# Key-value products and remainder rows moved into other runs of the TensorE stream (linear attention and a gated feed-forward on one core)

## The chip, the cores and the metric

The kernel runs on one core of a Trainium2 chip. The core has a matrix engine (TensorE, PE in the profile, with PEld for its weight loads), a vector engine (VectorE, DVE), a scalar engine (ScalarE, ACT), a general engine (GpSimd, POOL), a queue engine that mostly issues transfers (SyncE, SP), and 16 DMA engines that all queues share. The metric is the device time of one execution in microseconds (us), lower is better. Measured times are medians of several executions; a profile is one execution of its own.

## The reference

Eight batches, eight heads, 576 positions, 64 elements per head. Each batch and head computes a linear attention, is normalized over its 64 elements, and all 4608 rows of 512 then go through a normalized, gated feed-forward layer of width 1536:

```
kv  = einsum('bhsd,bhse->bhde', k, v)
out = einsum('bhsd,bhde->bhse', q, kv)
x   = out / sqrt(mean(out*out, -1) + 1e-6) * g_norm      # per head, then (b, s, h*d)
xn  = x / sqrt(mean(x*x, -1) + 1e-6) * rms_g             # per row
y   = (silu(xn @ w_gate) * (xn @ w_val)) @ w_out
```

Inputs and output are float32; the kernel multiplies in bfloat16 and sums in float32.

## The kernel before

**Tiling.** The 576 rows of a batch are cut into 512 main rows (`MAIN`, four chunks of 128, `NC = 4`) and a remainder of 64 (`REM`). The feed-forward works on eight groups of main rows, one per batch, and on one group of the 8 x 64 remainder rows. In its order the group of the remainder rows stands before that of the last batch. Code counts batches from 0 (`b`, `g`); the words here count from 1.

**A group** has 24 slots of its first half, gate and value in turn for each of the 12 column blocks `j` (`gate_of`, `val_of`, four matmuls of 512 columns each through `mm1`, L762), and 16 slots of its second half (`slots_b`, three matmuls each, L811). ACT applies silu to a gate (L771), DVE multiplies it with the value (L783), ACT copies the result of the second half (L831) and SP stores it (L833). The slots are the frame: `Placer.put` books the attention work of the next batch into the slots of the current group by estimated costs per engine, and `emit` writes out slot by slot. Each engine then runs its own instructions in that order, and waits only for semaphores.

**Attention of batch b** (`place_attention`, L669) is booked into group `b-1` (from 0): the transpose of q by SP (`qT_dma`, L381, and L384 for a pair of remainders), the k-v products on PE (`kv_mm`, L294, 40 matmuls whose results take half of the columns), their copy to `kvs` by DVE (`kv_half`, L324), o on PE (`o_heads`, L422, 32 matmuls that contract over half of the rows). Then come ACT's square and copy of o (`sq_`, `outa_`), POOL's weighted square (`wsq`, L514), DVE's sums (`red`, L522), a chain of twelve small DVE operations (`chain`, L562 to L580) that gives the scale `al`, the scaling (`xna_`, L591) and the transposes of x by SP (`x_dma`, L653) into the tile that the next group reads.

**Remainders.** The o of two batches' remainders is one more chunk (`o_rem`, L397) in the run of o of batches 3, 4, 6 and 8, with its squares and copies in halves (L405, L410), and a fifth column in the chain. The k-v products of batches 5 and 6, and of 7 and 8, form one run of 80 in the second half of the group before.

**PSUM** has three pools of tiles: `mm1` with three buffers, `o2` with two, `att` with three. A matmul that opens a tile waits until the last reader of its buffer is done.

**Loads.** POOL issues the loads of k and v with a cast (`load_cast`, L196 and L200) into two buffers each (`kc`, `vc`), SP those of q (`load_q`), which POOL or ACT casts. All waits of POOL and SP are in the order of their queues.

**The first two batches** are written out by hand. Batch 1's rows are made in two parts: its first group runs on the early half, while the late half is still scaled. `behind(n)` adds to the early slot `n`; at `n == 9` PE turns the late rows (L621) and ACT copies them out (L631). Batch 2 (`place_second`) sits in the first group's second half: four matmuls `oT` (L472), their squares on ACT (`sqT_`, L483), and sums over heads by small matmuls with a selection matrix (`stat_mm`, L507, four per `j`), then a chain on DVE (`lead_chain`) that scales its o.

Of the kernel before, what the change touches and what calls it, by code (L numbers as in the profile page):

```python
# [87 lines left out]
def kernel(  # L88
# [38 lines left out]
    xna_p = pool("xna", 2)  # L127
    x_p = pool("x", 3)
# [30 lines left out]
    q01r = consts.tile([2 * REM, H, D], BF16, name="q01r")  # L159
# [29 lines left out]
    def load_cast(b, t, heads=None):  # L189
        to = qc if t == 0 else (vc if t == 2 else kc)[b % 2]  # L190
        if heads is None:
            if t == 0:
                to = q01r[b * REM : (b + 1) * REM]
# [69 lines left out]
    class Att:  # L263
        def __init__(self, b):
            self.b = b
            self.kv, self.qT = kvs[b % 2 if b else 2], qTs[b % 2]
            self.chunks = NC + (b == 2 or b > 2 and b % 2)
            if b < 2:
                self.qTj = self.qT.rearrange("p c j t -> p (c j t)").rearrange("p (j c t) -> p j c t", j=NS, c=NC + 1)
            else:  # L270
                self.qTj = self.qT.rearrange("p c j t -> p j c t")
# [49 lines left out]

        def kv_half(self, half):
            rows, cols = slice(half * D, (half + 1) * D), slice(half * D, (half + 1) * D)
            nc.vector.tensor_copy(out=self.kv[rows, :, half, :], in_=self.kv_ps[rows, :, cols])  # L324
# [54 lines left out]
        def qT_dma(self):  # L379
            flat = mains[self.b, 0].rearrange("p c h d -> p (c h d)")  # L380
            nc.sync.dma_start_transpose(out=self.qT[:, 0:NC].rearrange("p c j t -> p (c j) t"), in_=flat)  # L381
            if self.chunks > NC:
                rem = q01r if self.b == 2 else rems[0][self.b // 2 % 2]
                nc.sync.dma_start_transpose(out=self.qT[:, NC], in_=rem.rearrange("p h d -> p (h d)"))  # L384

        def o_rem(self):

            of = (kvs[2], kvs[1]) if self.b == 2 else (kvs[0], kvs[1])
            self.o[NC] = [
                pool_.tile([128, H // 2, D], FP32, name=name) for pool_, name in ((att_p, "att"), (mm1_p, "mm1"))  # L390
            ]
            for j in range(NS):
                for n in range(2):
                    at = slice(n * REM, (n + 1) * REM)
                    for half in range(2):
                        rows = slice(half * D, (half + 1) * D)
                        nc.tensor.matmul(  # L397
                            self.o[NC][half][at, j, :], lhsT=self.qTj[rows, j, NC, at],
                            rhs=of[n][rows, j, half, :], start=True, stop=True, skip_group_check=True,
                        )  # L400

        def sq_rem(self, half):
            if NC not in self.sq:
                self.sq[NC] = sq_p.tile([128, 2, H, D], BF16, name="sq")
            nc.scalar.activation(out=self.sq[NC][:, 0, half:H:2, :], in_=self.o[NC][half], func=ACT.Square)  # L405

        def outa_rem(self, half):
            if NC not in self.outa:
                self.outa[NC] = outa_p.tile([128, H, D], BF16, name="outa")
            nc.scalar.copy(out=self.outa[NC][:, half:H:2, :], in_=self.o[NC][half])  # L410

        def o_heads(self):
# [5 lines left out]
            for c in range(NC):  # L418
                for j in range(NS):
                    for half in range(2):  # L420
# [3 lines left out]
                            rhs=self.kv[rows, j, half, :], start=True, stop=True, skip_group_check=True,  # L424
# [4 lines left out]
        def part(self, t, n):  # L429

            if n >= NC:
                return t[:, n]
# [12 lines left out]
        def xna_pairs(self, o, js, c0, c1):  # L445
            if not hasattr(self, "xna"):
                self.xna = xna_p.tile([128, NC + 1, H, D], BF16, name="xna")
# [6 lines left out]
        def o_of(self, c):  # L454
            return self.o[c] if c >= NC else self.o["main", c].rearrange("p c h d -> p (c h) d")
# [47 lines left out]
        def stat_mm(self, c0, c1):  # L503
            self.st = st = att_p.tile([128, 2, NC + 1, H], FP32, name="att")
            for c in range(c0, c1):
                for j in range(NS):
                    nc.tensor.matmul(  # L507
                        st[:, :, c, 2 * j : 2 * j + 2], lhsT=self.sqT[:, j, c], rhs=sel,
                        start=c == c0 and j == 0, stop=c == c1 - 1 and j == NS - 1,
                        skip_group_check=True,  # L510
                    )

# [3 lines left out]
        def red(self, c, which):  # L516
            if self.st is None:
                self.st = stat.tile([128, 2, NC + 1, H], FP32, name="st")
            of = self.sq[c][:, which]
            if c < NC:  # L520
                of = of.rearrange("p (c h) d -> p c h d", c=2)
            nc.vector.reduce_sum(out=self.part(self.st[:, which], c), in_=of, axis=AX.X)  # L522

        def chain_t(self):
            if not hasattr(self, "al"):
                t = lambda n, dt=FP32, h=H: stat.tile([128, NC + 1, h], dt, name=n)
                self.u, self.r, self.t, self.z, self.nt, self.al = (t(n) for n in ("u", "r", "t", "z", "nt", "al"))
                self.s = stat.tile([128, NC + 1], FP32, name="srow")
# [57 lines left out]
        def xna_(self, c, eng):  # L586
            if not hasattr(self, "xna"):
                self.xna = xna_p.tile([128, NC + 1, H, D], BF16, name="xna")
            if c < NC:
                of = self.o["main", c] if self.b == 1 else self.outa[c].rearrange("p (c h) d -> p c h d", c=2)  # L590
                return eng.tensor_tensor(  # L591
                    out=self.part(self.xna, c), in0=of,
                    in1=self.part(self.al, c).to_broadcast([128, 2, H // 2, D]), op=OP.mult,
                )
            return eng.tensor_tensor(
                out=self.xna[:, c], in0=self.outa[c], in1=self.al[:, c, :].to_broadcast([128, H, D]), op=OP.mult
# [48 lines left out]
        def x_dma(self, c0, c1):  # L645
# [3 lines left out]
            else:  # L649
                b = self.b // 2 * 2 if self.b > 2 else 0  # L650
                to = xr[:, :, b * REM : (b + 2) * REM]
                of = self.xna[:, NC].rearrange("p h d -> p (h d)")
# [16 lines left out]
    def place_attention(P, b, casts=(), at=0, chain_at=0, mate=None):  # L669
# [3 lines left out]
        N1 = range(a.chunks)  # L673
        P.floor = max(P.floor, at)
        load = P.put("SP", 0.0, a.qT_dma, casts[:1] if b == 2 else casts)
        qt = [("DMA", load[1] + QT_SLOTS)]
        if kv is None:
            of = [a] + ([Att(mate)] if mate else [])
            p = P.psum(1.2, lambda: [o.kv_mm(ALL) for o in of], casts, len(of))
            out_ = [[P.put("DVE", 0.4, lambda o=o, h=h: o.kv_half(h), [p]) for h in range(2)] for o in of]  # L680
            for tile_, ops in zip(P.tiles[-len(of) :], out_):
                tile_ += ops
            kv = out_[0]
            if mate:
                ahead[mate] = of[1], out_[1]
        else:
            P.floor = max(P.floor, start + 2)
        outs, reds = {}, []
        rem = a.chunks - NC
        main = P.psum(0.73 + 0.25 * rem, a.o_heads, kv + qt, 2 + rem)  # L690
        for c in (*N1[NC:], *N1[:NC]):
            if c == NC:
                for n in (1, 0):
                    s = P.put("ACT", 0.38, lambda n=n: a.sq_rem(n), [main])
                    outs[c] = P.put("ACT", 0.38, lambda n=n: a.outa_rem(n), [main])
                P.tiles[-1] += [s, outs[c]]
            else:
                s = P.put("ACT", 0.6, lambda c=c: a.sq_(c), [main])
                outs[c] = P.put("ACT", 0.6, lambda c=c: a.outa_(c), [main])
                if c >= 2:  # L700
                    P.tiles[c - NC - rem] += [s, outs[c]]
            assert outs[c][1] < start + 2 * NF, (b, outs)
            w = P.put("POOL", 1.2, lambda c=c: a.wsq(c, nc.gpsimd), [s])
            reds.append(P.put("DVE", 0.68, lambda c=c: a.red(c, 0), [s]))
            reds.append(P.put("DVE", 0.68, lambda c=c: a.red(c, 1), [w], w[1] + 3 * (b == 2)))
        prev = reds
        for n in range(0, 13, 4):
            prev = [P.put("DVE", 0.8, lambda n=n: [f() for f in a.chain(0, a.chunks)[n : n + 4]], prev, chain_at)]
        xn = [P.put("DVE", 0.68, lambda c=c: a.xna_(c, V), prev + [outs[c]]) for c in N1]
        put = [P.put("SP", 0.0, lambda c=c: a.x_dma(*c), [xn[c[1] - 1]]) for c in ((0, 2), (2, 4), (4, 5))[: a.chunks - 2]]  # L710
        return put[2 if b == B - 1 else 1][1] + X_SLOTS

    def place_second(P, s):
# [24 lines left out]
        P.at("PE", 0.5, lambda: a.stat_mm(0, NC), s + 5)  # L738
# [34 lines left out]
    def gate_of(g, j, c0=0, c1=MAIN):  # L773
        silu_of(g, j, mm1(g, wg, j, c0, c1, "o2" if g == 0 and c0 == 0 and j == 5 else "mm1"), c0, c1)
# [231 lines left out]
    G.memset(kvs[0], 0.0)  # L1006
# [20 lines left out]
    def behind(n):  # L1027
# [99 lines left out]
```

## Time and profile before

| | |
|---|---|
| median of 3 runs | 317.39 us (317.2 to 317.48) |
| profiled execution, its own time | 317.45 us |
| its span, first to last instruction | 315.7 us |
| granted TensorE clock | 1.000 |
| PE busy | 310.6 us, 98% of the span |
| DVE, ACT, POOL busy | 167.6, 139.1, 87.4 us |
| read from and written to memory | 37.78 MB, 9.44 MB |

The profile's page lists busy time by engine, the chain of work that ended last (followed back from the last instruction, at each step to what released it), and the costliest groups of instructions by source line. The chain can also be shown in order of time: start, length, engine, tile and line, with neighbouring pieces of the same line merged and their number behind an x. The timeline shows instructions of each engine with start, length and, in brackets, the idle time before them and what ended it. Matmuls are pipelined, so their starts are spaced more closely than they are long; the chain shows the spacing. For a DMA the landing is the time from issue to arrival.

### The profile page before, as it was taken

To read this page: it belongs to the slowest core of one execution; us is meant where nothing else is said; L and a number is where in the kernel's file an instruction comes from. 1 tells how busy PE (TensorE), PEld (TensorE's weight loads), DVE (VectorE), ACT (ScalarE), POOL (GpSimd) and SP (SyncE) were. 2 spreads that over 40 slices of the span, in tenths; PEclk is the share of its full clock that TensorE was granted. 3 is DMA by queue.
4 is the path that set the end of the run, shared out by engine and by line. 5 is a ranking of instruction groups with operands and counts; after the bars stand their busy time and mean duration, and the time that the engine had idled before them with its cause. 6 is when DMAs were issued, how large, how long until landed. Compare 5 with 4: busy or idle time off the path is not lost.

```text
span 315.7 us, 5706 instructions
## 1 busy us (share of the span) xinstructions
PE 310.6 (98%) x2220; PEld 154.8 (49%) x2220; DVE 167.6 (53%) x375; ACT 139.1 (44%) x261; POOL 87.4 (28%) x108
## 2 busy tenths in 40 slices
PE   8999999999999999999999999999999999999996
PEld 3688655544444445444444454444444444444444
DVE  4585456579669643955196638570769034103410
ACT  2374474595487324632483228322842233233321
POOL 8846430077068205830081007100510000000000
PEclk9999999999999999999999999999999999999999
DMA  9999999999899968997423444424001600040002
GB/s 199 194 203 199 196 237 200 192 231 147 190 162 215 179 152 140 253 175 163 166 85 67 94 135 141 83 48 152 3 0 25 194 1 0 21 105 9 2 33 100
DMA packets 78358, 40.18 MB, mean 127 GB/s; under 512 B 43000, under 2 KB 73852, under 8 KB 78332
## 3 DMA queue, kind: packets, MB, share of 16 engines
q0 software_dynamic: 32304, 14.75, 36.5%
q1 hardware_dynamic: 45328, 24.48, 31.6%
q10 hardware_dynamic: 700, 0.59, 0.6%
q8 instruction: 17, 0.28, 0.3%
q14 instruction: 9, 0.07, 0.1%
HBM read 37.78 MB, written 9.44 MB: 150 GB/s over the span
## 4 chain that ended last, share of the span: by engine, by line
PE 94%; DMA 2%; DVE 1%; POOL 1%; issue 1%; ACT 0%; DVEq 0%; POOLq 0%
PE mm L762 58%; PE o L811 27%; DMA vc<-in_v_dram 2%; PE mm L811 2%; PE att L294 2%; PE o L422 1%; PE o L842 1%; PE att L422 1%; PE att L472 1%; DVE h L783 0%; PE att L621 0%; PE mm L804 0%; PE o L762 0%; PE att L397 0%; PE mm L312 0%
## 5 line engine op out<-in xcount | busy, mean ns | idle before, releaser
L783 DVE TENSOR_TENSOR h<-silu,mm 128x512 bf16<-128x512 bf16 (+1 forms) x114 | 73.9, 650 | 101.1 <-PE mm L762 92.4
L771 ACT ACTIVATE silu<-mm 128x512 bf16<-128x512 f32 (+1 forms) x115 | 65.1, 570 | 83.5 <-PE mm L762 73.1
L762 PE MATMUL mm<-x,wv 128*128 128x512 bf16 (+1 forms) x408 | 97.7, 364 | 0.0
L762 PE MATMUL mm<-x,wg 128*128 128x512 bf16 (+1 forms) x404 | 97.5, 364 | 0.1
L811 PE MATMUL o<-wo,h 128*128 128x512 bf16 x396 | 89.6, 379 | 0.0
L762 PEld LDWEIGHTS <-wv 128*128 128x128 bf16 x468 | 45.1, 98 | 46.2
L762 PEld LDWEIGHTS <-wg 128*128 128x128 bf16 x456 | 44.4, 98 | 47.5 <-issue 0.4
L811 PEld LDWEIGHTS <-h 128*128 128x128 bf16 x420 | 40.6, 98 | 47.6
L514 POOL TENSOR_TENSOR sq<-sq,g 128x512 bf16<-128x512 bf16 x28 | 32.0, 1155 | 99.1 <-ACT sq L405 67.4
L831 ACT COPY osb<-o 128x512 f32<-128x512 f32 x33 | 19.3, 587 | 68.7 <-PE o L811 66.7
L522 DVE TENSOR_REDUCE st<-sq 128x8 f32<-128x512 bf16 x56 | 35.9, 678 | 0.0
L591 DVE TENSOR_TENSOR xna<-outa,al 128x512 bf16<-128x512 bf16 x24 | 15.1, 684 | 0.0
L324 DVE CAST kvs<-att 64x256 bf16<-64x256 f32 x14 | 5.9, 422 | 16.8 <-PE att L294 16.6
L200 POOL DMA_DIRECT2D kc<-in_k_dram x7 | 6.5, 924 | 29.0 <-PE att L294 26.1
L762 PE MATMUL mm<-xr,wg 128*128 128x512 bf16 x48 | 12.3, 379 | 0.0
L762 PE MATMUL mm<-xr,wv 128*128 128x512 bf16 x48 | 12.3, 379 | 0.0
L229 POOL CAST main_q<-stg 128x1024 bf16<-128x1024 f32 x10 | 10.1, 1043 | 1.2 <-DMA stg<-in_q_dram 1.2
L929 ACT ACTIVATE wv<-wv,gain 128x384 bf16<-128x384 bf16 x16 | 9.0, 607 | 0.4 <-PE mm L762 0.4
L200 POOL DMA_DIRECT2D vc<-in_v_dram x10 | 8.5, 857 | 2.1 <-PE att L294 1.1
L258 PE MATMUL mm<-idle 128*128 128x512 bf16 x20 | 7.2, 533 | 1.2 <-DVE idle L138 1.2
L811 PE MATMUL mm<-wo,h 128*128 128x512 bf16 x24 | 7.6, 379 | 0.0
L459 ACT ACTIVATE sq<-att 128x512 bf16<-128x512 f32 x12 | 7.5, 626 | 0.0
(151 smaller groups left out, 190.1 us busy)
## 6 DMA issues: line engine op xcount, KB each, us to landing
out_dram<-osb SPq DMA_DIRECT2D x27, 256.0 KB, 2.5
stg<-in_q_dram SPq DMA_DIRECT2D x6, 1024.0 KB, 11.2
vc<-in_v_dram POOLq DMA_DIRECT2D x7, 512.0 KB, 13.1
kc<-in_k_dram POOLq DMA_DIRECT2D x7, 512.0 KB, 7.8
out_dram<-osb SPq DMA_DIRECT2D x17, 128.0 KB, 2.4
wg<-in_moe_w_gate_dram POOLq DMA_DIRECT2D x4, 384.0 KB, 10.1
wv<-in_moe_w_val_dram POOLq DMA_DIRECT2D x4, 384.0 KB, 11.3
wo<-in_moe_w_out_dram POOLq DMA_DIRECT2D x4, 384.0 KB, 14.4
```

The source lines that it names most:

```text
L200: return nc.gpsimd.dma_start(out=to[:, heads[0] : heads[1], : NC * D], in_=view)
L229: return copy(out=mains[b, t][:, cs[0] : cs[1], h0:h1, :], in_=staged[b, t].rearrange("p h (c d) -> p c h d", c=NC)[:, cs[0] : cs[1], h0:h ...
L459: nc.scalar.activation(out=self.sq[c][:, 0], in_=self.o_of(c), func=ACT.Square)
L514: eng.tensor_tensor(out=self.sq[c][:, 1], in0=self.sq[c][:, 0], in1=g2, op=OP.mult)
L522: nc.vector.reduce_sum(out=self.part(self.st[:, which], c), in_=of, axis=AX.X)
L591: return eng.tensor_tensor(out=self.part(self.xna, c), in0=of, in1=self.part(self.al, c).to_broadcast([128, 2, H // 2, D]), op=OP.mult,)
L762: nc.tensor.matmul(ps[:, : c1 - c0], lhsT=w[n][:, s, jj * 128 : (jj + 1) * 128], rhs=x_of(g, s, c0, c1), start=s == 0, stop=s == NS - 1)
L771: nc.scalar.activation(out=sis[g, j][:, c0:c1], in_=ps, func=ACT.Silu)
L783: nc.vector.tensor_tensor(out=hs[g, j][:, c0:c1], in0=sis[g, j][:, c0:c1], in1=v_ps, op=OP.mult)
L811: nc.tensor.matmul(ps, lhsT=hs[g, j][:, t * 128 : (t + 1) * 128], rhs=wo[j // OB][:, j % OB, :], start=j == 0, stop=j == NF - 1)
L831: (eng.copy if eng is nc.scalar else eng.tensor_copy)(out=o, in_=ps)
L929: A.mul(out=w[:, s], in_=w[:, s], mul=gain[:, s : s + 1])
```

## The change

- The k-v products of batches 5 and 6 go into the runs of o of batches 4 and 5, those of 7 and 8 into the run of o of batch 6. The tile of batch 8 is taken from `mm1`. Every batch has its own `kvs` tile, from batch 3 on without the empty halves.
- The run of o of batch 4 moves from slot 3 to slot 11 of its group. That of batch 3 moves one slot ahead.
- The o of all remainders is done in two runs: those of batches 1 to 4 in the run of o of batch 7, of 5 to 8 in that of batch 8. Two pairs share two whole tiles, so that ACT squares and copies them in whole tiles. The q of each pair has a tile of its own (`qTr`), as has the scaled remainder (`rna`). The chain of batches 7 and 8 is written twice, for the main rows and for the remainders; in batch 8 the remainders come first.
- The loads of k and v of batch 5 are booked into group 2 (slot 34), those of batch 6 at slot 14 of group 3 where they stood at slot 0.
- The late rows of batch 1: two of the four copies go to DVE. Gate `j = 7` of the early half takes an `o2` tile.
- The sums of batch 2 are made in steps, right behind the `oT` matmuls, and not in one run of 16.

The diff, cut to its core:

```diff
-    kvs = [consts.tile([128, NS, 2, D], BF16, name=f"kvs{n}") for n in range(3)]
-    qTs = [consts.tile([128, NC + 1, NS, 128], BF16, name=f"qTs{n}") for n in range(2)]
+    kvs = [consts.tile([128, NS, 2, D] if n < 2 else [128, NS, D], BF16, name=f"kvs{n}") for n in range(B)]
+    qTs = [consts.tile([128, NC, NS, 128], BF16, name=f"qTs{n}") for n in range(2)]
+    qTr = [consts.tile([128, NS, 128], BF16, name=f"qTr{n}") for n in range(B // 2)]
...
-            self.chunks = NC + (b == 2 or b > 2 and b % 2)
+            self.rems = {6: (0, 1), 7: (2, 3)}.get(b, ())
+            self.chunks = NC + len(self.rems)
...
-        def kv_mm(self, js):
+        def kv_mm(self, js, pool=None):
             if not hasattr(self, "kv_ps"):
-                self.kv_ps = att_p.tile([128, NS, 2 * D], FP32, name="att")
+                self.kv_ps = (pool or att_p).tile([128, NS, 2 * D], FP32, name="mm1" if pool is mm1_p else "att")
...
         def o_rem(self):
...
+            for half, (pool_, name) in enumerate(((att_p, "att"), (mm1_p, "mm1"))):
+                self.o["main", NC + half] = pool_.tile([128, 2, H // 2, D], FP32, name=name)
+            for i, r in enumerate(self.rems):
+                for j in range(NS):
+                    for n in range(2):
+                        at = slice(n * REM, (n + 1) * REM)
+                        for half in range(2):
+                            rows = slice(half * D, (half + 1) * D)
+                            nc.tensor.matmul(
+                                self.o["main", NC + half][at, i, j, :], lhsT=qTr[r][rows, j, at],
+                                rhs=Att(2 * r + n).kv_of(rows, j, half), start=True, stop=True, skip_group_check=True,
+                            )
...
         if kv is None:
-            of = [a] + ([Att(mate)] if mate else [])
-            p = P.psum(1.2, lambda: [o.kv_mm(ALL) for o in of], casts, len(of))
...
+            p = P.psum(0.85, lambda: a.kv_mm(ALL), casts)
+            kv = halves(a, p)
+            P.tiles[-1] += kv
+            if mates:
+                P.floor = max(P.floor, start + 10)
         else:
             P.floor = max(P.floor, start + 2)
...
+        def products():
+            a.o_heads()
+            for o, pool_ in zip(of, (None, mm1_p)):
+                o.kv_mm(ALL, pool_)
...
-        main = P.psum(0.73 + 0.25 * rem, a.o_heads, kv + qt, 2 + rem)
+        main = P.psum(0.73 + 0.25 * len(a.rems) + 0.65 * len(of), products, kv + qt, 2 + rem + bool(of))
...
+        mains, rests = (0, NC), (NC, a.chunks)
+        for c0, c1 in (rests, mains) if b == B - 1 else (mains, rests)[: 1 + rem]:
+            prev = [r for c in range(c0, c1) for r in reds[c]]
+            for n in range(0, 13, 4):
+                prev = [P.put("DVE", 0.8, lambda n=n, c0=c0, c1=c1: [f() for f in a.chain(c0, c1)[n : n + 4]], prev, chain_at)]
...
-        P.at("PE", 0.5, lambda: a.stat_mm(0, NC), s + 5)
+        for j in range(NS):
+            P.at("PE", 0.11, lambda j=j: a.stat_pairs((j,), 0, NC, att_p, "att"), s + (3, 4, 4, 5)[j])
...
-        silu_of(g, j, mm1(g, wg, j, c0, c1, "o2" if g == 0 and c0 == 0 and j == 5 else "mm1"), c0, c1)
+        silu_of(g, j, mm1(g, wg, j, c0, c1, "o2" if g == 0 and c0 == 0 and j in (5, 7) else "mm1"), c0, c1)
...
-    G.memset(kvs[0], 0.0)
...
-                    a.xT_out(j, (2, 3), A)
+                    a.xT_out(j, (2, 3), A if js is P0 else V)
...
+            for f in loads_kv(b + 2):
+                P.put("POOL", 0.85, f, at=starts[1] + 34)
...
-            end = place_attention(P, b, casts, s0 - 2, s0 + 2 * NF - 4, b + 1 if b in (4, 6) else None)
+            end = place_attention(P, b, casts, s0 - 2, s0 + 2 * NF - 4, {3: (4,), 4: (5,), 5: (6, 7)}.get(b, ()))
...
-            P.put("SP", 0.0, lambda b=b: load_q(b + 1), at=starts[b - 1] + 6 * (b == 2))
+            P.put("SP", 0.0, lambda b=b: load_q(b + 1), at=starts[b - 1] + 6 * (b < 4))
...
-            for of, at in {3: ((5, 0), (4, 14)), 4: ((6, 0), (7, 14))}.get(b, ()):
+            for of, at in {3: ((5, 14),), 4: ((6, 0), (7, 14))}.get(b, ()):
```

More of the change, by code (lines that the diff above doesn't have):

```diff
@@ L386, in o_rem @@
         def o_rem(self):
[L388 to L400, printed above, removed]
@@ L501, in stat_pairs @@
                     first = False
[L503 to L511, printed above, removed]
         def wsq(self, c, eng):
@@ L587, in xna_ @@
             if not hasattr(self, "xna"):
[L588 to L594, printed above, removed]
+                self.xna = xna_p.tile([128, NC, H, D], BF16, name="xna")
+            if c == NC:
+                self.rna = rna_p.tile([128, 2, H, D], BF16, name="rna")
+            of = self.o["main", c] if self.b == 1 else self.outa[c].rearrange("p (c h) d -> p c h d", c=2)
             return eng.tensor_tensor(
-                out=self.xna[:, c], in0=self.outa[c], in1=self.al[:, c, :].to_broadcast([128, H, D]), op=OP.mult
+                out=self.part(self.xna, c) if c < NC else self.part(self.rna, c - NC), in0=of,
+                in1=self.part(self.al, c).to_broadcast([128, 2, H // 2, D]), op=OP.mult,
             )
@@ L676, in place_attention, with halves @@
         qt = [("DMA", load[1] + QT_SLOTS)]
+        def halves(o, p):
+            return [P.put("DVE", 0.4, lambda o=o, h=h: o.kv_half(h), [p]) for h in range(2)]
         if kv is None:
[L678 to L682 removed]
@@ new lines, in place_attention @@
+        rem, of = bool(a.rems), [Att(n) for n in mates]
+        def products():
+            a.o_heads()
+            for o, pool_ in zip(of, (None, mm1_p)):
+                o.kv_mm(ALL, pool_)
+        base = len(P.tiles)
+        main = P.psum(0.73 + 0.25 * len(a.rems) + 0.65 * len(of), products, kv + qt, 2 + rem + bool(of))
+        for n in reversed(range(len(of))):
+            ahead[mates[n]] = of[n], halves(of[n], main)
+            if n == 0:
+                P.tiles[-1] += ahead[mates[n]][1]
@@ L706, in place_attention @@
[L706 to L711, printed above, removed]
+            reds[c] = [
+                P.put("DVE", 0.68, lambda c=c: a.red(c, 0), [s]),
+                P.put("DVE", 0.68, lambda c=c: a.red(c, 1), [w], w[1] + 3 * (b == 2)),
+            ]
@@ L713, in place_second @@
+        return ends[NC if b == B - 1 else 2] + X_SLOTS
     def place_second(P, s):
```

84 lines of the change are left out of this document (34 added, 50 removed).

## The prediction

> **What bounds the kernel now.** I read the page's totals first, then the list of PE's waits, then the chain that ended last, and at the places that the change touches the timeline.
>
> ```profile
> span 315.7 us, 5706 instructions
> PE 310.6 (98%) x2220; PEld 154.8 (49%) x2220; DVE 167.6 (53%) x375; ACT 139.1 (44%) x261; POOL 87.4 (28%) x108
> ...
> PE 94%; DMA 2%; DVE 1%; POOL 1%; issue 1%; ACT 0%; DVEq 0%; POOLq 0%
> ```
>
> ```profile
> PE mm L258 <- DVE idle L138: 1.2, 1, 1.2
> ```
>
> PE carries 94% of the chain. That row is the longest of PE's waits, and like the three shorter ones behind it in the list it is of the opening. DVE and ACT are about half busy and reach the path only through something that PE waits for. A change can therefore gain by less PE time, or lose by a new PE wait. PE's instructions are the same 2220 after as before, in another order, so what can be gained is what the order costs. The chain, from the second half of group 2 through the first of group 4, shows this:
>
> ```profile
> 76.60 9.71 PE o L811 x45
> 86.31 0.75 PE att L294 x40
> 87.06 0.75 PE o L811 x3
> 87.82 2.59 PE mm L762 x12
> 90.41 0.34 PE o L422 x16
> 90.75 0.23 PE att L422 x16
> 90.98 0.14 PE att L397
> ...
> 91.23 18.23 PE mm L762 x84
> 109.47 9.71 PE o L811 x45
> 119.18 1.39 PE att L294 x80
> 120.56 0.75 PE o L811 x3
> 121.32 2.59 PE mm L762 x12
> 123.91 0.34 PE o L422 x16
> 124.25 0.23 PE att L422 x16
> 124.48 18.24 PE mm L762 x84
> ```
>
> A wide matmul takes 9.71/45 = 0.2158 us, so 48 take 10.36. Those from 76.60 to 87.82 took 11.22 with 40 k-v products (L294) among them: these cost 0.86. From 109.47 to 121.32, 80 of them cost 11.85-10.36 = 1.49. So 40 products are 0.63 of work, and 0.23 per run is the price of entering and leaving it, 0.115 a border. From 121.32 to 142.72 (124.48+18.24), 96 wide matmuls (20.72) and the o of one batch (L422) took 21.40: 0.68, or 0.45 of work and two borders. From 87.82 to 109.47, with the remainders' o (L397), it is 0.93: 0.25 more, 0.14 of work and one border more.
>
> **The change part by part.** Batches are counted from 1, as is the group of feed-forward slots that each feeds.
>
> *Runs of k-v and o.* Before, the ten runs of batches 3 to 8 have 24 borders: four k-v runs with two each, two o runs with two, four o runs with remainders with three. After: k-v 3, o 3 and k-v 4 have two each; o 4 with k-v 5, o 5 with k-v 6, o 6 with k-v 7 and 8, o 7 and o 8 with two remainders each have three. That makes 21. The work is the same, so PE saves 3 x 0.115 = 0.35. The border straight from o to k-v is not in the trace. The nearest row is that from 64x64 turns (L359) to k-v:
>
> ```profile
> 39.04 0.75 PE att L294 x40
> ```
>
> There 40 products, right behind the turns of batch 2, took 0.75 up to their last: 0.63 and a border of 0.12. I take 0.115. If it were free, the three merged runs would save 0.35 more; if it cost twice as much, the saving would vanish. [...]
>
> *Late rows of the first batch.* Before, the PE stream stumbles here:
>
> ```profile
> 22.86 1.57 ACT L631 ACTIVATE x<-att,gain 128x256 bf16<-128x256 bf16 x4 [1.15 <-PE att L621]
> ...
> 23.04 2.31 PE L762 MATMUL mm<-x,wg 128*128 128x256 bf16 x16
> ...
> 23.23 0.74 DVE L783 TENSOR_TENSOR h<-silu,mm 128x256 bf16<-128x256 bf16 x2
> 23.70 0.86 PEld L762 LDWEIGHTS <-wg 128*128 128x128 bf16 x8 [0.24 <-issue]
> 23.89 0.41 DVE L783 TENSOR_TENSOR h<-silu,o 128x256 bf16<-128x256 bf16 x1
> ...
> 24.75 0.31 PEld L762 LDWEIGHTS <-wg 128*128 128x128 bf16 x3 [0.19 <-issue]
> ...
> 25.18 0.60 PE L762 MATMUL mm<-x,wv 128*128 128x256 bf16 x4
> ```
>
> Four gates of 4 matmuls run from 23.04 to 25.18, 2.14 us for 16 x 0.109 = 1.75. The lost 0.4 is two holes: at 23.70 gate j=7 waits for an mm1 buffer that a product frees at 23.64, at 24.75 the first late gate for one that the silu behind ACT's four copies frees. After, j=7 takes an o2 buffer long free, and two copies go to DVE, so both holes close. But the late gate reads what DVE copies: its order puts them behind the product of 23.89, at 24.22 (DVE starts one every 0.33 here) and about 24.5, 0.34 each as below, so the last is there at 24.84 and the fourth matmul starts at about 24.9 and ends at 25.0. That is 0.18 before 25.18. The bounds are 0 (DVE late by as much) and 0.4. I take 0.15. The added DVE wait stands ahead of everything on PE, so its length counts in full.
>
> ```profile
> L633 DVE TENSOR_SCALAR x<-att,gain x9: 341/341/352, 17.1 to 52.5; 128x256 bf16<-128x256 bf16 x9
> ```
>
> *Second batch's statistics.* 16 small matmuls in one run become runs of 4, 8 and 4.
>
> ```profile
> 17.69 0.08 PE att L497 x4
> ...
> 44.21 0.52 PE att L507 x16
> 44.73 0.45 PE o L811 x2
> ```
>
> Two wide matmuls are 0.43, so 44.73 is 0.02 long: 16 cost 0.54. With as much behind them, four cost 0.10 where a wide matmul stands ahead, and four times that is 0.40: a gain of 0.14. The last step still waits for the last square:
>
> ```profile
> 43.60 0.60 ACT L483 ACTIVATE sqT<-att 128x512 bf16<-128x512 f32 x1 [0.27 <-PE att L472]
> ```
>
> It is 0.1 later after, since four small matmuls now stand before the one that feeds it, and so ends at 44.30; PE arrives at 44.35. Bounds: -0.1 (a wait) and 0.14. I take 0.10.
>
> *What lies beside PE.* The split of the chain of small DVE operations adds 24 of them; they stand in the second halves of groups 6 and 7, where DVE has little else, and the remainder group lies between the last of them and its reader. ACT evacuates remainders in 8 whole tiles in place of 16 halves, about the same time. K-v 8 holds one of three mm1 buffers until DVE has copied it, and PE asks for that one again two slots (1.7 us) later. The o runs of batch 3, one slot earlier, still come behind its copies of k-v. One memset less on POOL frees 0.55. SP issues as many transposes as before. I cost all of these at nothing; if that cover were gone, each would show as a PE wait of its length.
>
> *What is moved.* In POOL's queue the loads of batch 5 move from slot 14 of group 3 to slot 34 of group 2 (there POOL has only casts of q before them), those of batch 6 from slot 0 to slot 14 of group 3, behind the products for batch 4 and in part behind casts of q; those of batch 7 follow straight on, since their buffer is free as soon as k-v 5 is done. I estimate the last eight at 103 to 112. They pass no wait that PE needs. On PE the o of batch 4 goes from slot 3 of group 3 (90.41) to slot 11: group 3 begins at 87.3 (0.25 for the remainders' o gone from group 2, 0.25 for the opening), eleven slots of 0.863 end at 96.8, the run takes 1.43. After it come 13 slots (11.2), to 109.4, and the second half (10.36): group 4 begins at 119.8. For batch 5 the scaling of x now begins 1.05 after the first half's end (124.48+18.24 against the row below), which would be 110.5. After, DVE has only those 12 us for eight sums of 0.68 (5.4), seven products, two copies and the chain, so I allow 0.7 more: 111.2. The first transpose of x issues 1.3 later (two scalings of 0.62), the second 2.5 after it, behind a store, as the rows show: 112.5 and 115.0.
>
> ```profile
> L522 DVE TENSOR_REDUCE st<-sq 128x8 f32<-128x512 bf16 x56 | 35.9, 678 | 0.0
> ```
>
> ```profile
> 143.77 2.49 DVE L591 TENSOR_TENSOR xna<-outa,al 128x512 bf16<-128x512 bf16 x4
> ```
>
> ```profile
> 111.97 1.81 SPq L653 DMA_TRANSPOSE x<-xna  x1
> ...
> 114.52 1.29 SPq L653 DMA_TRANSPOSE x<-xna  x1
> ```
>
> The view of the tile x has the landings of all 12:
>
> ```profile
> DMA to landing us min/median/max: 3.0/3.2/3.3
> ```
>
> At 3.2 us the second lands at 118.2, 1.6 before its reader; now it is 114.52+3.2 = 117.7 against 121.32, 3.6 before. For group 3 the scaling comes earlier than now, since its chain and a fifth chunk no longer stand in the second half, and x with it. So I cost the move at nothing, with half the room gone.
>
> The sum: 0.35+0.15+0.10 = 0.60. The profiled execution took 317.45, 1.75 around its span, 0.06 above the median of the runs, 317.39. It becomes 316.85; beside the median 316.8.
>
> **The rivals.**
>
> *Slower: x of group 4 is late.* The transposes would run beside 2 batches of k-v loads. No x transpose of the trace did that for long, but q's, twice as long, did:
>
> ```profile
> L381 SPq DMA_TRANSPOSE qTs<-main_q x6: 1379/3254/4763, 51.5 to 197.9; - x6
> ...
> DMA to landing us min/median/max: 4.4/7.2/8.2
> ```
>
> Of the six, those beside loads land in 7 to 8 us and the others in 4.4, and the issue on SP takes 4.7 for 1.4. By the ratio of the median to the least, 1.6, x lands in 5.2, and the first transpose may hold SP up to 2 us longer. Then PE waits 0.4 (115.0+5.2-119.8) to 2.4 at the head of group 4. It decides from a landing of 4.8 us onward, and makes the change slower by 0.2% from a wait of 1.2. Middle of that case: 318.3. Against it: at 111.97 SP took 1.81 and the landing stayed in its narrow range. [...]
>
> *Only the borders pay.* DVE's copies come as late as ACT's did, and the statistics wait for the square: 0.35 less, 317.05. For it: ends of 24.84 and 44.30 that leave 0.05 to 0.2.
>
> *A k-v product waits for its loads inside an o run.* The loads of batch 6, issued until about 109, are wanted at 123 (three slots into group 4 and behind o).
>
> ```profile
> vc<-in_v_dram POOLq DMA_DIRECT2D x7, 512.0 KB, 13.1
> ```
>
> At 13.1 they are there at 122; a few us more stall PE by as much, to some 318.5. Against it: no q load starts beside them.
>
> *The border from o to k-v is free:* 316.5.
>
> **How the numbers follow.** My forecast, 316.8 with 316.55 to 317.0 of its own, has 0.53; the borders alone 0.17; the free border 0.06; late x 0.17; late loads 0.07. A measurement here can tell some 0.2%, 0.63 us, from no change: 316.75 is that line, just under my value, so 0.53 divides nearly evenly. Faster 0.36: 0.27 of the forecast, the free border and a little of the others. Same 0.44: the rest of the forecast, the borders alone, the milder part of late x. Slower 0.20: the rest of late x and of late loads. The range goes from 316.4 to 318.2, which leaves out the longest stalls.
>
> **What the profile after would show.** The chain should have 1.43 for o with k-v 5 or 6 and its borders, 1.07 for o with two remainders, no k-v run inside the second halves of groups 3 and 5; the run of 16 gate matmuls 1.75 plus about 0.2; statistics 0.08 to 0.1 for four. No PE wait at the head of group 4, with x transposes at about 112.5 and 115.0. A wait there, SP issues of 2 us and more, or a PE wait named k or v inside an o run would make me wrong.

## The result, and the profile after

The changed kernel takes 331.93 us (median of 6 runs, 330.96 to 334.57) against 317.44 us before (317.14 to 317.59). The ratio is 1.047, with a 95% interval of 1.043 to 1.051: 14.5 us slower. The forecast was 316.8 with a range to 318.2.

The page of the profiled execution after: span, PE's share, and the shares of the chain that ended last.

```profile
span 330.1 us, 5721 instructions
PE 314.4 (95%) x2220; PEld 155.6 (47%) x2220; DVE 172.0 (52%) x401; ACT 137.9 (42%) x251; POOL 86.8 (26%) x107
...
PE 83%; DMA 9%; DVE 5%; issue 1%; POOL 1%; SPq 0%; ACT 0%; DVEq 0%; POOLq 0%
```

DMA has gone from 2% of the chain to 9%, and PE from 94% to 83%. The list of PE's waits says which transfer (total, times, longest):

```profile
PE mm L755 <- DMA x<-xna: 10.9, 2, 6.4
```

Two waits, 4.5 and 6.4 us, both on the transposed x, at the heads of groups 3 and 4; the list's two other rows, 1.2 and 0.2 us, are of the opening. In the chain in order of time, each landing is followed by matmuls that take too long:

```profile
81.61 9.96 DMA x<-xna
91.62 11.69 PE mm L755 x44
...
121.00 11.73 DMA x<-xna
132.77 4.69 PE mm L755 x12
```

At the full clock 44 wide matmuls take 44 x 0.2158 = 9.50 and 12 take 2.59. These took 2.19 and 2.10 more. The table by windows shows why (window, PE busy, granted clock, DMA share, GB/s):

```profile
86.00:88.00 2.00, 1.16 (x29) 1.00 1.33 182
88.00:90.00 2.00, 0.00 (x0) 0.73 1.40 232
90.00:92.00 2.00, 0.38 (x1) 0.50 1.22 283
92.00:94.00 2.00, 2.00 (x6) 0.50 1.04 297
94.00:96.00 2.00, 2.00 (x6) 0.56 1.10 355
96.00:98.00 2.00, 2.00 (x11) 1.00 0.68 142
```

The clock falls to half while PE waits and comes back some 4 us after it has started again. So 10.9 of waiting and 4.3 of slow matmuls are 15.2 us; the span grew by 14.4, and the other 0.8 us is what the change saves.

Why x is late is in the queues. On SP, the transposes of q, of a pair of remainders, and then the two of x for group 3:

```profile
73.44 3.62 SPq L387 DMA_TRANSPOSE qTs<-main_q  x1
77.16 1.75 SPq L391 DMA_TRANSPOSE qTr<-remq  x1
79.19 1.44 SPq L633 DMA_TRANSPOSE x<-xna  x1
...
81.61 4.58 SPq L633 DMA_TRANSPOSE x<-xna  x1
```

On POOL, the first and last of the four loads of batch 5, and, for group 4, the first of the four of batch 6 and the last of the four of batch 7:

```profile
73.92 0.95 POOL L201 DMA_DIRECT2D kc<-in_k_dram  x1
...
76.41 0.71 POOL L197 DMA_DIRECT2D vc<-in_v_dram  x1
...
109.26 0.95 POOL L201 DMA_DIRECT2D kc<-in_k_dram  x1
...
118.00 0.74 POOL L197 DMA_DIRECT2D vc<-in_v_dram  x1
```

The two transposes of x for group 3, before:

```profile
81.53 1.23 SPq L653 DMA_TRANSPOSE x<-xna  x1
...
83.48 1.29 SPq L653 DMA_TRANSPOSE x<-xna  x1
```

So x is issued in time: for group 3 it goes out 2 us earlier than before. For group 4 it goes out at 118.94 and 121.00; less the 6.6 us that the first stall cost, that is 112.3 and 114.4, where it was 111.97 and 114.52. But a batch of loads is under way at group 3, two at group 4. The view of tile x gives the landings after issue, for all 12 transposes; before, they lay between 3.0 and 3.3:

```profile
DMA to landing us min/median/max: 3.1/6.2/11.7
```

### The profile page after: what moved, and what is told of

Its sections match the earlier page's. It is cut to its first block, busy times and chain, and to the rows that moved or that the text cites. A ratio compares the mean times of both kernels' runs of the same rounds, so it can differ in the third digit from the quotient of the medians.

```text
span 330.1 us, 5721 instructions
## 1 busy us (share of the span) xinstructions
PE 314.4 (95%) x2220; PEld 155.6 (47%) x2220; DVE 172.0 (52%) x401; ACT 137.9 (42%) x251; POOL 86.8 (26%) x107
## 4 chain that ended last, share of the span: by engine, by line
PE 83%; DMA 9%; DVE 5%; issue 1%; POOL 1%; SPq 0%; ACT 0%; DVEq 0%; POOLq 0%
PE mm L755 55%; PE o L804 20%; DMA x<-xna 7%; DMA vc<-in_v_dram 2%; PE mm L804 2%; DVE xna L574 1%; DVE h L776 1%; PE att L296 1%; PE o L418 1%; PE o L835 1%; PE o L755 1%; PE att L418 1%; PE att L466 0%; POOL vc L201 0%; PE att L601 0%
## 5 line engine op out<-in xcount | busy, mean ns | idle before, releaser
L776 DVE TENSOR_TENSOR h<-silu,mm 128x512 bf16<-128x512 bf16 (+1 forms) x114 | 73.9, 649 | 115.8 <-PE mm L755 114.3
L755 PE MATMUL mm<-x,wg 128*128 128x512 bf16 (+1 forms) x400 | 99.3, 372 | 10.9 <-DMA x<-xna 10.9
L755 PE MATMUL mm<-x,wv 128*128 128x512 bf16 (+1 forms) x408 | 99.5, 369 | 0.0
L330 DVE CAST kvs<-att 64x256 bf16<-64x256 f32 x12 | 5.1, 421 | 9.4 <-PE att L296 9.3
L453 ACT ACTIVATE sq<-att 128x512 bf16<-128x512 f32 x14 | 8.7, 620 | 0.0
L457 ACT CAST outa<-att 128x512 bf16<-128x512 f32 x14 | 8.6, 613 | 0.0
```

The source lines that it names most:

```text
L453: nc.scalar.activation(out=self.sq[c][:, 0], in_=self.o_of(c), func=ACT.Square)
L755: nc.tensor.matmul(ps[:, : c1 - c0], lhsT=w[n][:, s, jj * 128 : (jj + 1) * 128], rhs=x_of(g, s, c0, c1), start=s == 0, stop=s == NS - 1)
L776: nc.vector.tensor_tensor(out=hs[g, j][:, c0:c1], in0=sis[g, j][:, c0:c1], in1=v_ps, op=OP.mult)
```

## The experiments

Four explanations were open: the loads stretch x (A); the transposes of q, ahead of x in SP's queue, hold it up (B); the new order of work on PE and DVE makes x itself late (C); and, after the first runs, whatever is issued ahead of x on any queue shares the engines with it (D). Ratios are to the kernel before on the same chip, whose median was 317.15 to 317.75.

### Loads held back until x has landed

```diff
-                P.put("POOL", 0.85, f, at=starts[1] + 34)
+                P.put("POOL", 0.85, lambda f=f: behind_x(f, 2), at=starts[1] + 34)
...
+    def behind_x(f, b):
+        tc.add_manual_dep(f().ins, last_x[b].ins.name, SYNC, reason="x comes first")
```

The same is done for the loads of batch 7 with x of group 4; those of batch 6 follow directly on those of batch 5.

> The changed kernel, with the loads of batch 5 issued only when both transposes of x for group 3 have landed, those of batch 6 right behind them, and those of batch 7 only when both transposes of x for group 4 have landed. Theory A (the k-v loads in flight stretch the transposes of x): x lands in about 3.2 us at groups 3 and 4, the waits of 4.5 and 6.4 us on x and the slow matmuls behind them go, and the time falls from 331.9 to 316.8, or up to 319 if the loads of batch 5, issued at about 85, come late for its k-v products at 97. Theory B (the transposes of q and of the remainders, ahead of x in SP's queue, hold x up): those are as before, so the waits stay and the time is about 332. Theory C (the new order of work on PE and DVE makes x itself late): likewise about 332.

320.93 us, ratio 1.012 (1.010 to 1.013), 2 us above the range of theory A. x of groups 3 and 4 lands in 3.0 to 3.2 us and both waits on it are gone, with q and PE's order as they were. B alone and C alone are out. The k-v products of batch 5 now wait for their late v instead, inside the run of o:

```profile
PE att L296 <- DMA vc<-in_v_dram: 2.7, 2, 1.5
```

The first and last of batch 5's loads went out at 85.00 and 87.50, and PE waited at 97 and again at 98.8. These waits and slow matmuls behind them (1.3 us) make up the 4 us by which the run stays above 316.8. A further run held back only the loads of batch 7:

> The changed kernel, with only the loads of batch 7 held back until x for group 4 has landed; batch 5 and batch 6 load as they did. Theory A: the wait at group 3 stays at 4.5 us; at group 4 half of the bytes in flight are gone, so that the landing of the second transpose falls from 11.7 to some 5 to 8 us and the wait from 6.4 to 0 to 3; 325 to 330 in all. Theories B and C: both waits stay, 332.

323.57 us, ratio 1.020 (1.018 to 1.022), below the 325 to 330 expected. With one batch of loads ahead of it in place of two, x of group 4 lands 4.7 and 4.3 us after issue in place of 9.0 and 11.7, and its wait is gone; the wait of group 3 is still 4.4. So each wait has its own loads behind it, and at group 4 the loads of batch 7, which in the changed kernel follow straight on those of batch 6, make the difference.

### Half of the bytes, and q out of the way

One kernel leaves out the k half of batch 5's loads (`loads_kv(b + 2)[2:]`), the other puts the transposes of q for batches 4 and 5 behind those of x:

```diff
-        load = P.put("SP", 0.0, a.qT_dma, casts[:1] if b == 2 else casts)
+        load = P.put("SP", 0.0, a.qT_dma, casts[:1] if b == 2 else casts, {3: starts[1] + 32, 4: starts[2] + 32}.get(b, 0))
```

> The changed kernel without the k half of the loads of batch 5 (its k-v products use the k of batch 3 that still lies in the buffer: that part of the output is another): half of the bytes in flight ahead of x for group 3. Theory A: those loads end some 6 us earlier, at about 84, the wait of 4.5 at group 3 falls to 0 to 1 and the slow matmuls behind it with it; group 4 is unchanged; 325 to 327. Theory B: unchanged, 332.

> The changed kernel, with the transposes of q for batches 4 and 5 (and the first of the remainders) put behind those of x in SP's queue; all loads as they were. Theory A: the loads still fill the engines, x still lands 8 to 11 us after its issue, waits of 3 to 6 us at both groups, 329 to 332. Theory B: x lands in about 3.2 us and the waits go, 317 to 319.

Half the bytes: 325.41 us, ratio 1.026 (1.024 to 1.028). x of group 3 lands in 6.3 and 6.0 us, at 86.9, just as PE gets there; at group 4 it still waits 6.8. As A has it.

q behind x: 324.19 us, ratio 1.022 (1.020 to 1.024). Here A was wrong: with all loads in flight, the wait at group 3 is gone too. The second transpose of x lands 5.0 us after issue:

```profile
DMA to landing us min/median/max: 5.0/5.0/5.0
```

At group 4, where two batches of loads are ahead, the same edit doesn't help: landings of 9.0 and 10.5, a wait of 5.4. So neither the loads nor q alone make x late at group 3; together they do. The loads of batch 5 themselves landed at 90.8 with q beside them, and at 84.0 without. That is theory D: one pool of engines works off what has been issued. Whether it does so in turn or side by side, these runs don't show.

### Another queue for x, and the loads alone in the kernel before

Theory D was tried in two ways. In the changed kernel the four transposes of x for groups 3 and 4 were issued from ACT:

```diff
-            return nc.sync.dma_start_transpose(out=to, in_=of)
+            return (nc.scalar if c0 < NC and 2 <= self.b <= 3 else nc.sync).dma_start_transpose(out=to, in_=of)
```

> The changed kernel, with the four transposes of x for groups 3 and 4 issued from ACT's queue; the transposes of q stay on SP's, ahead in time. Theory D (one pool of engines, no matter which queue): x still lands 8 to 11 us after its issue, waits of 4 to 7 us at both groups, 330 to 334. Theory B in its narrow form (x waits behind the transposes of q because they are in the same queue): x passes them and lands in 3 to 5 us, the wait at group 3 goes, 320 to 325.

333.62 us, in two runs 5 us apart, so the time isn't used. At group 4, q had landed at 125.7 and x went out from ACT at 125.75, with SP's queue empty of transposes. It landed in 9.6 and 10.1 us: two batches of loads ahead do that to x from ACT's queue as from SP's. At group 3 the run says nothing on D, since ACT didn't issue x until 87.18, right when the remainders' q had landed at 87.1:

```profile
87.18 1.33 ACTq L633 DMA_TRANSPOSE x<-xna  x1
88.63 0.58 ACT L824 COPY osb<-o 128x512 f32<-128x512 f32 x1 [8.81 <-issue]
```

At both groups it went out within 0.1 us of a landing of q; why ACT held it until then, the run doesn't show. Behind it ACT's copies stood still, the one in the row above for 8.81 us, and PE waited 8.6 us for them. The second queue was no way out here.

In the kernel before, only the loads of batch 5 (and, by its slot, batch 6) were moved to where the change has them:

> The kernel before, with only the loads of batch 5 moved to where the change puts them (group 2, slot 34) and those of batch 6 to slot 14 of group 3; the work of PE, DVE and ACT is as before. Theory D (what is issued ahead of x on any queue shares the 16 engines with it: the k-v loads and the transposes of q together make x late): the loads go out at about 77 to 80, beside the transposes of q at 76, x for group 3 lands at 92 to 94 in place of 86.8, PE waits some 4 to 6 us and has slow matmuls for 2 more: 323 to 326. Theory C (PE's and DVE's new order makes x late): no wait, 317.2.

325.96 us, ratio 1.026 (1.024 to 1.028). x of group 3 lands 10.4 and 7.8 us after issue, at 94.0, and the wait is there without any other part of the change:

```profile
PE mm L762 <- DMA x<-xna: 6.2, 1, 6.2
```

At group 3 the move of the loads is enough to make x late; nothing else of the change is needed for it. x of group 4 lands in 3.1 us in this run: there the loads of batch 7 don't follow on those of batch 6, but go out behind x, from 129 on.

### Are the slow matmuls PE's own?

So far every long wait had crowded transfers beside it. In the kernel before, each scaling of x for group 3 was done three times over (`[a.xna_(c, V) for _ in range(3 if b == 2 else 1)]`), to delay x without any transfer:

> The kernel before, with each scaling of x for group 3 done three times over on DVE (5 us more DVE work ahead of its transposes, no transfer more or longer). x lands some 5 us later, at 91.7, and PE waits 3.5 to 4.5 us at the head of group 3. If the slow matmuls behind the waits of the changed kernel come from PE's own pause, they appear here too and cost 1.5 to 2.5 us more: 322 to 324. If they come from the crowded transfers, the matmuls behind this wait run at full speed: 320.5 to 322.

330.65 us, ratio 1.042 (1.040 to 1.044). This missed, and showed D once more: delayed to 89.09, the second transpose fell among the loads of batch 6, issued from 87.43 on, and landed 9.4 us later. PE waited 10.6 us. The question was asked again in the last kernel of the next part, which has no loads there, with the scaling four times over:

> That kernel, with each scaling of x for group 3 done four times over (7.2 us more of DVE ahead of the transposes), in a stretch where no k-v loads are under way. x lands in 3.2 us, at 91 to 92, and PE waits 4 to 5 us. If the slow matmuls behind the long waits come from PE's own pause, the 44 matmuls behind it lose about 2.2 us; if they come from the crowded transfers, they lose nothing.

323.85 us; x lands in 3.1 us, PE waits 5.1, and the 44 matmuls behind it take 12.25 in place of 9.50, 2.75 more:

```profile
88.86 3.06 DMA x<-xna
...
91.96 12.25 PE mm L768 x44
```

```profile
88.00:90.00 2.00, 0.00 (x0) 1.00 0.00 0
90.00:92.00 2.00, 0.04 (x1) 0.60 1.07 254
92.00:94.00 2.00, 2.00 (x5) 0.50 0.99 191
94.00:96.00 2.00, 2.00 (x6) 0.50 0.83 171
96.00:98.00 2.00, 2.00 (x7) 0.69 1.01 278
```

Other transfers are under way behind this pause too (q and its transposes, DMA share 0.83 to 1.07). But crowded engines alone don't lower the clock: in the run with all loads behind x, PE worked at the full clock beside a DMA share of 1.35:

```profile
104.00:106.00 2.00, 2.00 (x11) 1.00 1.35 151
```

So the pause itself halves the clock (from 1.00 to 0.50 here, with no k-v loads under way). Pauses of 4.5 to 10.6 us in these runs lost 2.1 to 2.8 us each in the wide matmuls right behind them, and one of 1.0 lost at most 0.2. The delay is not the same each time: read in windows of half a microsecond, the clock fell 1.8 us after PE had stopped at the first wait of the changed kernel, and 3.6 us at its second. At these two waits and in this run it was back 3.9 to 5.3 us after PE had started again.

### Is the saving there, with x in time?

First, the late rows and the statistics alone, on the kernel before:

```diff
-        silu_of(g, j, mm1(g, wg, j, c0, c1, "o2" if g == 0 and c0 == 0 and j == 5 else "mm1"), c0, c1)
+        silu_of(g, j, mm1(g, wg, j, c0, c1, "o2" if g == 0 and c0 == 0 and j in (5, 7) else "mm1"), c0, c1)
...
-                    a.xT_out(j, (2, 3), A)
+                    a.xT_out(j, (2, 3), A if js is P0 else V)
...
-        P.at("PE", 0.5, lambda: a.stat_mm(0, NC), s + 5)
+        for j in range(NS):
+            P.at("PE", 0.11, lambda j=j: a.stat_pairs((j,), 0, NC, att_p, "att"), s + (3, 4, 4, 5)[j])
```

> The kernel before with only two edits of the change: the late rows shared by DVE and ACT with gate 7 in an o2 buffer, and the second batch's statistics in steps. The prediction's terms for these two: 0.15 and 0.10, so 316.9 where the kernel before is at 317.15; the rows of the changed kernel's trace speak for 0.3 to 0.5, 316.65 to 316.85. If they only shift a wait, 317.15.

317.05 us, ratio 0.998 (0.997 to 0.999), some 0.6 us. The timeline of PE at the late rows:

```profile
22.44 0.61 PE L621 MATMUL att<-ident,xna 128*128 128x128 bf16 x8
...
24.81 0.60 PE L763 MATMUL mm<-x,wv 128*128 128x256 bf16 x4
```

From the turns to the first value they take 2.37 us, before 25.18-22.43 = 2.75. In the profiled execution the k-v products of batch 3 then wait 0.3 for their v, so that part of it is given back there: its span is 315.6, its own time 317.42, one of the longest of the 11 runs. Whether the shorter ones had that wait, no trace shows.

Then the whole change, with q for batches 4 and 5 behind x and the loads of batch 7 behind x of group 4:

> The changed kernel, with the transposes of q for batches 4 and 5 behind those of x in SP's queue, and the loads of batch 7 held back until x for group 4 has landed. Theory D: at group 3 x lands in about 5 us, as it did with q behind alone; at group 4 only the loads of batch 6 are ahead of x, issued by 109, and x lands in 3 to 5 us; no wait at either group, no slow matmuls, and what is left is the sum of the prediction: 316.3 to 316.8. If the new order of the products itself costs time, it stays above 317.15.

318.01 us, ratio 1.001 (1.000 to 1.002): a miss. x of group 4 lands in 3.2 to 3.4 us and costs nothing, but the second one of group 3 lands in 5.9, and 1.0 us of wait is left. Next the loads of batch 5 went ahead of POOL's casts of q, from 74 to 71:

> As the last of the runs before (q for batches 4 and 5 behind x, the loads of batch 7 behind x of group 4), and the loads of batch 5 issued ahead of the casts of q, at about 71 in place of 74. By theory D the second transpose of x for group 3, which landed at 88.1 there and cost a wait of 1.0 us, lands at about 85.5, ahead of its reader at 87.2; no wait on x is left, and the time is 0.5 to 1.2 us under the kernel before. If the landing does not follow the loads, the wait of 1.0 stays.

318.00 us, ratio 1.002 (1.001 to 1.003). x lands in 3.2 us, at 86.4, and no wait on it is left, as D said (though x also went out 1 us later than in the run before). The forecast of the time missed; it stays because of a new wait:

```profile
PE o L810 <- DVE h L782: 1.0, 1, 1.0
```

In that kernel the casts run from 74.48 to 76.53, and DVE's chain beside them looks like this:

```profile
73.10 0.83 DVE L544 TENSOR_SCALAR u<-st 128x32 f32<-128x32 f32 x1
...
74.58 0.19 DVE L549 TENSOR_REDUCE srow<-t 128x4 f32<-128x32 f32 x1
74.80 0.81 DVE L550 SCALAR_TENSOR_TENSOR z<-srow,u 128x32 f32<-128x32 f32 x1
75.64 0.93 DVE L553 TENSOR_SCALAR y<-z 128x32 int32<-128x32 int32 x1
76.60 0.53 DVE L560 TENSOR_TENSOR nt<-y 128x32 f32<-128x32 f32 x1
```

The same with the late rows and statistics put back as they were:

> The first kernel of this set with the late rows and the statistics put back as they were: what is left is the new order of k-v and remainders, with loads that keep out of x's way. The prediction's term for it: 0.35 under the kernel before. If the border from o to k-v is free, 0.7; if a k-v product waits for its loads, the difference is lost or turns.

318.71 us, ratio 1.004 (1.002 to 1.005), but with the same wait of 1.0 on DVE and 0.8 of waits in the opening that the profile of before doesn't have. So it doesn't give the order's own worth. In the next run, which has the late rows and statistics again, the casts wait until DVE has scaled x:

```diff
+            def held_cast(hs):
+                tc.add_manual_dep(cast_main(b, 0, nc.gpsimd, hs).ins, last_xna[2].ins.name, SYNC, reason="the scaling comes first")
```

> As the kernel with the loads of batch 5 earlier, and POOL's casts of q for batch 4 held back until DVE has scaled x for group 3. There the casts ran from 74.5 to 76.5 beside DVE's chain, three operations of which took 0.5 to 0.9 us in place of 0.2 to 0.5, and PE waited 1.0 us for a product behind it. If the casts stretched the chain, its operations are back at 0.2 to 0.5, the wait of 1.0 goes, and the span falls from 316.2 to about 315.0, the time to 0.1 to 0.3% under the kernel before. If something else stretched it, the wait stays.

316.80 us, ratio 0.998 (0.997 to 0.999): 0.2% under the kernel before, and the lowest time of all that were run. The late rows and statistics alone had the same ratio, so the times don't resolve what the new order adds; only the traces do. The chain is back at its usual lengths, and the wait is gone:

```profile
72.98 0.17 DVE L544 TENSOR_SCALAR u<-st 128x32 f32<-128x32 f32 x1
...
74.03 0.19 DVE L550 SCALAR_TENSOR_TENSOR z<-srow,u 128x32 f32<-128x32 f32 x1
74.25 0.18 DVE L553 TENSOR_SCALAR y<-z 128x32 int32<-128x32 int32 x1
74.47 0.19 DVE L560 TENSOR_TENSOR nt<-y 128x32 f32<-128x32 f32 x1
```

The second transpose of x for group 3 lands 6.0 us after issue, at 86.8, just 0.2 before PE needs it: the room is nearly used up. The chain in order of time, at the points that answer to those quoted of before:

```profile
core 0 of [0], span 314.7 us
...
53.47 1.08 PE mm L768 x5
...
85.44 0.75 PE att L296 x40
86.19 0.75 PE o L817 x3
86.94 9.51 PE mm L768 x44
...
109.38 10.09 PE o L817 x46
119.47 2.59 PE mm L768 x12
```

## Why the prediction was wrong

**The sum was there.** The kernel with the casts held back has the forecast's own conditions, x in time, so its terms can be read beside the kernel before. By its time the saving is 0.2%, 0.3 to 1.0 us, which the forecast of 0.60 fits; by one trace of each, the terms were rather too small:

| term | forecast | measured | read from |
|---|---|---|---|
| late rows | 0.15 | 0.35 to 0.38 | 22.43 to 25.18 before; 22.28 to 24.68, and 22.44 to 24.81 in the run alone |
| statistics | 0.10 | 0.11 | 16 in 0.54 before; 4, 8 and 4 in 0.11, 0.20 and 0.12 |
| remainders' o out of group 2 | 0.25 | 0.26 | first half of group 2 to the head of group 3: 54.09 to 87.82, 53.47 to 86.94 |
| the rest of the order | 0.10 | 0.12 | from there to the end: 227.88 and 227.76 us |

With 0.15 of the opening, which no edit explains, that is the 1.0 us between the spans of 315.7 and 314.7. The borders at 0.115 held: a run of o with k-v 6 cost 1.43 in the first kernel with q and batch 7 behind x (120.86 to 143.01 less 96 wide matmuls), o with two remainders 1.05 in the changed one (1.07 forecast). The late rows were mis-sized on the safe side: I let DVE's copies start at 24.22 or later, and in the run alone they started at 23.96.

**The step that failed is the price of the moved loads**: that they "pass no wait that PE needs", that x for group 3 comes earlier with its scaling ("and x with it"), and so "I cost the move at nothing". No wait of PE's stands in POOL's queue, but the landings of x depend on what else the 16 engines carry (3.0 to 3.3 us before, 9.0 to 11.7 here at groups 3 and 4), and PE waits for those: 10.9 us, and 4.3 more of slow matmuls. Loads beside x stood only in a rival, and only at group 4. For group 3 the prediction has no times at all of the loads of batch 5; they went out from 73.92 on, q at 73.44 and x at 79.19 and 81.61, and what they ask of the engines together was not added up. The trace of before had the parts. A batch of loads went out from 99.60 on, with the end of the loads of q and a transpose of q the only others beside it, and its last landed at 110.4, as the view of tile vc of the kernel before shows (issue at 102.1, 8.3 to the last landing). So a batch took 10.8 us from the first issue to the last landing:

```profile
L196 POOL DMA_DIRECT2D vc<-in_v_dram x1: 703/703/703, 102.1 to 102.1; - x1
...
DMA to landing us min/median/max: 8.1/8.2/8.3
```

A transpose of q is 4.4, one of x 3.2. An estimate by simple addition from the first issue of the loads gives 73.9+10.8+4.4+3.2 = 92.3 for x at group 3; it landed at 91.6. For half the bytes it gives 86.6 (86.9 measured), for the loads moved in the kernel before 95.0 (94.0). PE wants x at 87.2, so the sum says 5 us late. It is rough, and on the high side where more is in flight: with q behind x it gives 87.9 (86.2 measured), and for the two batches and q at group 4 138.5, where x landed at 132.7.

**The rival was right in kind and wrong in place and size.** "x of group 4 is late" named the mechanism with a chance of 0.17, at one group, with landings of 5.2 us by the ratio of 1.6 that q had shown, and a wait of 0.4 to 2.4. It happened at both groups, with landings of 9.0 to 11.7. q's ratio of 1.6 rests on transposes like that at 104.85, with one batch of loads beside it; x had a batch and q, or two batches and q, ahead of it. The issue times were right: in the run with q behind x, which has no stall at group 3, x of group 4 goes out at 112.31 and 114.50 (forecast 112.5 and 115.0), the loads from 102.6 to 111.4 (forecast 103 to 112).

**A wait was priced at its length.** The long ones cost 2.1 to 2.8 us more through the clock. No pause of the kernel before was long enough to show it; the longest was 1.2.

What the prediction named as signs against itself, a wait at the head of group 4 and SP issues of 2 us and more, both came (3.68 us at 121.00).

## What to carry to other kernels

Before a load is moved, write down everything that is on the way when the next transfer that PE needs goes out, from all queues, and add up how long each takes alone: the urgent one lands about when the sum is done (here within 2 us with one batch of loads ahead, 2 to 6 early with two), not after its own usual time. A queue's own waits say nothing on that. Order the transfers so that the urgent one goes first, and count a long pause of PE (those of 4.5 us and more showed it here) as 2 to 3 us longer than it is.

## What the runs showed of the hardware that I had not expected

- A transpose of x that takes 3.0 to 3.3 us alone took 8.9 to 12.1 behind two batches of loads, from SP's queue and from ACT's alike, and held SP for up to 3.9 us in place of 1.3; behind one batch and q it held SP for up to 4.6.
- Transposes of q and loads slow each other: the same four loads landed at 84.0 without q beside them and at 90.8 with it, and a transpose of q, 4.4 us at the least in the kernel before, landed in 7.1 there at 104.85, with a batch of loads beside it.
- Three small DVE operations beside casts on POOL (74.48 to 77.08 with that of the remainders) took 0.5 to 0.9 us in place of 0.2 (L550, L553 and L560, which lost 1.7 us), and holding the casts back took the stretch away (0.18 to 0.19 each). What stretched these and not L549, which took 0.19 at 74.58 beside the same casts, was not shown. L544 doesn't fit either: it took 0.83 us at 73.10, before the casts began, beside the issue of a load at 72.92; with the casts held back it took 0.17 beside the same issue. Why, the runs leave open.
- Two pauses of 1.5 and 1.2 us, 0.3 apart, lowered the clock like one long one (0.52 from 100 to 102 and 0.63 from 102 to 104 in the first experiment), and the 52 wide matmuls behind them took 12.50 in place of 11.22.
